# Retention attention followed by a GELU layer pair on one core: first layers of two blocks in token halves, finer activation sums, and POOL's scaling held until a block's sums are done

## The chip, the core and the metric

The kernel runs on one core of a Trainium2 chip. TensorE (PE in the profile) multiplies matrices, with its weight loads on PEld. VectorE (DVE), ScalarE (ACT) and GpSimd (POOL) do this kernel's elementwise work, and the sync engine (SP) issues most of its transfers (96 of the 144 loads of q, k and v; POOL's 48 are the tails). The metric is the time of one execution on the device in us, the median of several runs.

## The reference, cut to what matters

Inputs are q, k and v of 8 sequences, 8 heads, 576 positions and 64 dimensions. The attention is linear, with a causal mask and a decay per head. Its result, 4608 tokens by 512, goes through two layers.

```python
ret = (scale * q @ k.T) * Dmat          # Dmat[i, j] = gamma_h ** (i - j) for i >= j, else 0
x = (ret @ v), heads side by side       # (4608, 512)
h = x @ w_in                            # (4608, 2048)
out = gelu_tanh(h) @ w_out              # (4608, 512)
```

## The kernel before: the parts that the change touches

TensorE works through nine blocks (0 to 8) of 512 tokens. A block is 16 column groups of the first layer (`up`), then the second layer. From block 1 on, the second layer is done with seven products of half matrices instead of eight (`prod`), which needs sums of activations (`act_sums`, on DVE) and of weights (`weight_sums`). Attention work of later sequences is woven into the steps of the blocks. Nothing is rescheduled: each engine gets its instructions in the program's order (in block 2 DVE ran the copy L266 at 121.33 us, behind the sums L440 to L443, which the program has ahead of it and which began at 110.24).

```python
def up(t, fc):                                   # first layer, 512 tokens, 128 columns
    hp = bank("hp", "hp")
    for ct in range(4):
        nc.tensor.matmul(hp..., w_in_sb[:, ct, 128*fc : 128*fc+128], xT[:, o : o + 8, ct, :], ...)
    nc.scalar.activation(out=gT[t][:, fc]..., in_=hp, func=AF.Gelu_apprx_tanh)

def act_sums(t, f0, f1):                         # DVE; both inputs of each lie in SBUF
    nc.vector.tensor_tensor(out=s["1"], in0=a21, in1=a22, op=ALU.add)          # L440
    nc.vector.tensor_tensor(out=s["2"], in0=s["1"], in1=a11, op=ALU.subtract)  # L441
    nc.vector.tensor_tensor(out=a21, in0=a11, in1=a21, op=ALU.subtract)        # L442
    nc.vector.tensor_tensor(out=s["4"], in0=a12, in1=s["2"], op=ALU.subtract)  # L443

# ... blocks 1 on: the sums are issued inside a step, before that step's attention work
            for f in range(NH):
                steps.append(lambda f=f: up(t, f))
                def hi(f=f):
                    up(t, f + NH)
                    if f == 4:
                        act_sums(t, 0, 4)
                    if f == 7:
                        act_sums(t, 4, 8)
                steps.append(hi)
# ...
        for u, s in enumerate(steps):
            s()
            run(t, u)                            # the attention work planned for step u of block t

# scaling of k and q with the decay, on POOL, for sequence b: in block b - 2 from step 16 on
        at(t0, ut[0], lambda b=b: (new_casts(b), new_turned(b)))
        for u, (key, c) in zip(ut, ent):
            at(t0, u, lambda b=b, key=key, c=c, e=eng[key]: cc(b, key, c, e))
```

The "tail" of a sequence is its last 64 positions, loaded by six transfers that POOL issues itself (`load_tail`, L78) and scaled by two smaller products. In blocks 1 to 3 (sequences 1 to 3) transposed k and q come from TensorE through PSUM and are copied to `tt` by DVE (L266); later sequences are transposed by transfers.

## Time and profile before

335.8 us, median of 3 runs (335.27 to 335.86). From the timeline of TensorE, a "block" below lasts from its first first-layer matmul to that of the next block; block 0 counts from the start of the span.

| stretch | us | idle time of TensorE in it that matters |
|---|---|---|
| start and block 0 | 66.55 | 1.88 before the first layer; 1.57 and 2.06 between 41 and 47; 1.3 from 63 to 66.5 |
| block 1 | 33.61 | 0.78 |
| block 2 | 44.78 | 7.27 and 0.89 |
| blocks 3, 4, 5 | 31.61, 33.00, 31.69 | 0.59 in each of blocks 4 and 5 |
| blocks 6, 7, 8 | 32.09, 31.06, 30.81 | none |

The page of the profile, part 1 (busy us, share of the span, instructions) and two rows of part 2 (40 equal slices of 8.4 us, in tenths; PEclk is the granted clock):

```profile
PE 308.9 (92%) x2660; PEld 190.8 (57%) x2660; DVE 191.9 (57%) x303; ACT 167.7 (50%) x322; POOL 130.5 (39%) x175
...
PE   6969869899999748999999999999999999999994
...
PEclk9999998999999959999999999999999999999999
```

TensorE bounds the kernel: no other engine is near it on average. The time that a change could win is where its row is under 9: in five of the first eight slices, and in the 14th to 16th, above all in the 15th, where its busy share is 4 and the clock is 5 (the last slice is the end of the program). The timeline of 109.5 to 123.2 us shows that place (start, duration, engine, line, operation, result and inputs; in brackets the idle time before it and what ended it):

```profile
108.95 1.22 POOL L78 DMA_DIRECT2D lt<-in_v_dram  x2
...
110.18 1.05 POOL L232 TENSOR_TENSOR ck<-ld,sc 128x512 f16<-128x512 f32 x1
110.24 8.52 DVE L440 TENSOR_TENSOR s<-gT 128x1024 f16<-128x1024 f16 x1 [0.84 <-ACT gT L395]
...
111.18 1.05 POOL L232 TENSOR_TENSOR cq<-ld,sc 128x512 f16<-128x512 f32 x1
...
117.18 1.03 POOL L232 TENSOR_TENSOR cq<-ld,sc 128x512 f16<-128x512 f32 x1
118.18 1.05 POOL L232 TENSOR_TENSOR ck<-lt,sc 128x256 f16<-128x256 f32 x1
118.80 0.98 DVE L441 TENSOR_TENSOR s<-s,gT 128x1024 f16<-128x1024 f16 x1
...
121.33 0.68 DVE L266 COPY tt<-tr 128x1024 f16<-128x1024 f16 x1
...
122.06 0.61 PE L288 MATMUL st<-tt 64*128 64x128 f16 x8 [7.27 <-DVE tt L266]
```

Read it from the bottom: TensorE waited 7.27 us for a copy on DVE of 0.68 us. The copy was ready to go at 113, but stood behind four sums, the first of which lasted 8.52 us (the same group has a median of 0.69 in the view of that line). During all of it POOL ran its eight 128x512 products, one every 1.00 us. The wait does not end the loss, as the windows show (window, its length, then busy us and instruction counts of PE, PEld, DVE, ACT and POOL, then PEclk, DMA share and GB/s):

```profile
117.00:122.00 5.00, 0.00 (x0) 0.00 (x0) 4.96 (x5) 0.00 (x0) 5.00 (x7) 0.51 1.15 316
122.00:126.00 4.00, 3.94 (x24) 1.75 (x25) 1.63 (x4) 0.60 (x1) 0.67 (x2) 0.50 1.29 197
126.00:130.00 4.00, 4.00 (x35) 2.51 (x34) 0.97 (x2) 2.78 (x6) 1.23 (x2) 0.83 1.27 202
```

After the wait TensorE ran at half its clock for some five us: in narrower windows the clock is 1.00 from 114.80 to 117.08, 0.50 from 117.10 to 127.32 and 1.00 after, so it was halved 2.3 us into the wait and came back 5.3 us after work began again. Twelve first-layer matmuls took 4.90 us there (at 122.97), against 2.76 at full clock (at 108.54).

In blocks 3 to 5 the same sums meet the same POOL products, but there the two engines take turns: the timeline of DVE in block 4 has each sum at about twice its usual time (1.42 to 1.53 us for 0.69), and POOL's products beside them take 1.49 us instead of 1.04.

```profile
187.06 1.53 DVE L440 TENSOR_TENSOR s<-gT 128x1024 f16<-128x1024 f16 x1
188.62 1.42 DVE L441 TENSOR_TENSOR s<-s,gT 128x1024 f16<-128x1024 f16 x1
```

### The profile page before, as it was taken

Reading aid. Unit: us, or ns where it says so; the run is one execution under the profiler, and the core shown is the slowest. Engines: PE = TensorE matmul, PEld = TensorE weight load, DVE = VectorE, ACT = ScalarE, POOL = GpSimd, SP = SyncE. Lnnn points to the kernel's source line nnn. Section 1 sums busy time; section 2 is a strip of 40 time slices with the busy share of each in tenths; the row PEclk is TensorE's granted clock in tenths of the full one; section 3 lists DMA queues with packets and bytes.
Section 4 is the critical chain, followed back from the end, with each engine's and each line's share of the span. In section 5 each row is a group of like instructions: output and inputs, shape, how many; then the busy total and the mean of one; then the engine's idle time right before and its main releaser. Section 6 shows DMA issues by size and latency. Waiting matters only on the chain.

```text
span 335.2 us, 6603 instructions
## 1 busy us (share of the span) xinstructions
PE 308.9 (92%) x2660; PEld 190.8 (57%) x2660; DVE 191.9 (57%) x303; ACT 167.7 (50%) x322; POOL 130.5 (39%) x175
## 2 busy tenths in 40 slices
PE   6969869899999748999999999999999999999994
PEld 3634335444874326864684478447745864585483
DVE  4854477857554875646643964399345545651352
ACT  6466314778255505447735754674367246713610
POOL 8669368764594961008900980085000000000000
PEclk9999998999999959999999999999999999999999
DMA  8999999999999999875799597304410030003003
GB/s 206 220 349 367 295 248 222 207 236 217 199 215 182 204 269 194 169 203 119 177 192 207 133 177 133 125 2 79 127 63 2 2 124 5 0 2 125 2 0 127
DMA packets 123471, 51.30 MB, mean 153 GB/s; under 512 B 111920, under 2 KB 113968, under 8 KB 123440
## 3 DMA queue, kind: packets, MB, share of 16 engines
q1 hardware_dynamic: 121904, 47.72, 63.1%
q0 software_dynamic: 1536, 3.15, 4.2%
q8 instruction: 21, 0.34, 0.4%
q14 instruction: 10, 0.08, 0.1%
HBM read 36.70 MB, written 9.44 MB: 138 GB/s over the span
## 4 chain that ended last, share of the span: by engine, by line
PE 70%; DVE 12%; DMA 10%; SPq 3%; ACT 2%; issue 2%; POOL 1%; DVEq 0%
PE hp L389 27%; PE opB L458 12%; PE opC L458 9%; PE opA L458 7%; DVE s L440 4%; DMA ld<-in_moe_w_in_dram 4%; PE st L288 3%; PE xs L337 3%; PE op L407 3%; DMA ld<-in_q_dram 2%; SPq L90 2%; PE us L307 2%; DMA ld<-in_moe_w_out_dram 2%; DVE s L441 2%; PE xs L355 2%
## 5 line engine op out<-in xcount | busy, mean ns | idle before, releaser
L389 PE MATMUL hp<-xT,w_in_sb 128*128 128x512 f16 x576 | 135.0, 384 | 2.6 <-ACT xT L376 2.6
L395 ACT ACTIVATE gT<-hp 128x512 f16<-128x512 f32 x144 | 86.2, 598 | 76.0 <-PE hp L389 75.4
L389 PEld LDWEIGHTS <-w_in_sb 128*128 128x128 f16 x576 | 54.3, 99 | 62.5 <-issue 6.7
L232 POOL TENSOR_TENSOR ck<-ld,sc 128x512 f16<-128x512 f32 x31 | 36.4, 1175 | 75.5 <-PE us L307 37.0
L294 DVE TENSOR_TENSOR ret<-st,cm 128x512 f16<-128x512 f32 x64 | 41.2, 685 | 35.4 <-PE st L288 35.4
L458 PEld LDWEIGHTS <-gT 128*128 128x128 f16 x512 | 49.0, 98 | 7.2 <-issue 0.7
L458 PEld LDWEIGHTS <-s 128*128 128x128 f16 x384 | 36.3, 98 | 5.7 <-DVE s L441 1.1
L440 DVE TENSOR_TENSOR s<-gT 128x1024 f16<-128x1024 f16 x16 | 21.1, 1318 | 28.1 <-ACT gT L395 28.1
L328 ACT CAST tbd<-ws 64x256 f16<-64x256 f32 x64 | 25.8, 403 | 14.2 <-DVE ws L323 13.4
L458 PE MATMUL opB<-wt,gT 128*128 128x256 f16 x256 | 30.9, 273 | 0.5 <-DVE ost L472 0.5
L458 PE MATMUL opA<-w_out_sb,gT 128*128 128x256 f16 x256 | 31.0, 273 | 0.0
L232 POOL TENSOR_TENSOR cq<-ld,sc 128x512 f16<-128x512 f32 x24 | 28.1, 1171 | 0.8 <-DMA ld<-in_q_dram 0.6
L288 PE MATMUL st<-tt 64*128 64x128 f16 x288 | 15.2, 221 | 9.1 <-DVE tt L266 8.2
L337 PE MATMUL xs<-ret,cv 128*64 128x128 f16 x288 | 16.8, 225 | 4.8 <-DVE ret L294 3.6
L288 PEld LDWEIGHTS <-tt 64*128 64x128 f16 x288 | 8.2, 95 | 22.8 <-issue 10.0
L337 PEld LDWEIGHTS <-cv 128*64 128x64 f16 x288 | 10.3, 109 | 18.3 <-issue 16.6
L472 DVE TENSOR_TENSOR ost<-k,opC 128x512 f32<-128x512 f32 x16 | 11.0, 687 | 16.4 <-PE opC L458 16.1
L472 DVE TENSOR_TENSOR k<-k,opB 128x512 f32<-128x512 f32 x16 | 11.0, 686 | 15.6 <-PE opB L458 15.6
L376 ACT CAST xT<-xs 128x512 f16<-128x512 f32 x31 | 18.1, 582 | 2.0 <-PE xs L355 1.5
L219 ACT CAST cv<-ld 128x512 f16<-128x512 f32 x24 | 14.0, 616 | 6.5 <-PE xs L337 6.2
L407 PE MATMUL op<-w_out_sb,gT 128*128 128x512 f16 x64 | 16.9, 391 | 0.0
L514 DVE CAST w_out_sb<-ld 128x512 f16<-128x512 f32 x16 | 8.5, 551 | 14.3 <-DMA ld<-in_moe_w_out_dram 14.0
(83 smaller groups left out, 338.0 us busy)
## 6 DMA issues: line engine op xcount, KB each, us to landing
out_dram<-ost SPq DMA_DIRECT2D x17, 512.0 KB, 3.0
ld<-in_q_dram SPq DMA_DIRECT2D x32, 256.0 KB, 5.5
ld<-in_k_dram SPq DMA_DIRECT2D x32, 256.0 KB, 5.2
ld<-in_v_dram SPq DMA_DIRECT2D x32, 256.0 KB, 5.2
ld<-in_moe_w_in_dram SPq DMA_DIRECT2D x16, 256.0 KB, 5.7
ld<-in_moe_w_out_dram SPq DMA_DIRECT2D x16, 256.0 KB, 5.4
lt<-in_k_dram POOLq DMA_DIRECT2D x16, 64.0 KB, 4.5
lt<-in_q_dram POOLq DMA_DIRECT2D x16, 64.0 KB, 6.0
```

The lines of the kernel that those rows point to most:

```text
L232: eng.tensor_tensor(out=dst.rearrange("p (h d) -> p h d", d=D), in0=raw.rearrange("p (h d) -> p h d", d=D), in1=sc[:, s0 : s0 + nh].unsque ...
L288: nc.tensor.matmul(st[hl][:, 128 * p : 128 * p + 128], a["tk"][r, 4 * c + p, :], tq(b, c, p)[r], start=True, stop=True)
L294: nc.vector.tensor_tensor(out=r[:, 0:w], in0=st[hl][:, 0:w], in1=m.rearrange("p n i -> p (n i)"), op=ALU.mult)
L328: cp(out=tbd[b % 2][r, c, :, r], in_=att[b]["w"][r])
L337: nc.tensor.matmul(xs[64 * hl : 64 * hl + 64, 128 * p : 128 * p + 128], a["v"][:, col(c, p, hl)], a["ret"][c, hl][:, 128 * p : 128 * p + 128],
L376: nc.scalar.copy(out=xT[:, g0 : g0 + 2], in_=src)
L389: nc.tensor.matmul(hp.rearrange("p (g t) -> p g t", t=TL), w_in_sb[:, ct, 128 * fc : 128 * fc + 128], xT[:, o : o + TB // TL, ct, :], star ...
L395: nc.scalar.activation(out=gT[t][:, fc].rearrange("p i n -> p (i n)"), in_=hp, func=AF.Gelu_apprx_tanh)
L407: nc.tensor.matmul(op[i], gT[t][:, f, i], w_out_sb[:, f, :], start=(f == 0), stop=(f == NF - 1))
L440: nc.vector.tensor_tensor(out=s["1"], in0=a21, in1=a22, op=ALU.add)
L458: nc.tensor.matmul(op[tag][:, HD * u : HD * u + HD], lhs(f), rhs[:, f], start=(new and u == 0 and f == 0), stop=(f == NH - 1), skip_group_ ...
L472: nc.vector.tensor_tensor(out=o, in0=a, in1=b, op=ALU.add)
```

## The change

Its intent has three parts. Blocks 0 and 1 do their first layer for 256 tokens at a time, so that it can begin before the attention of all 512 tokens is done; the tail of sequence 0 and the chunks of sequence 1 are planned later to fit. The sums of activations are issued in four portions instead of two, after the step's attention work. For sequences 4 to 7, POOL first copies one element of the last sum of the current block (the gate), so that its products cannot start before the sums are done.

```diff
+    def up_half(t, u, f):                      # two column groups for 256 tokens, one bank
+        hp = bank("hp", "hp")
+        for x in range(2):
+            for ct in range(4):
+                nc.tensor.matmul(hp[:, 256*x : 256*x+256]..., w_in_sb[:, ct, 128*(f+x) ...], xT[:, o : o + 4, ct, :], ...)
+        nc.scalar.activation(out=gT[t][:, f : f + 2, 2*u : 2*u + 2, :]..., in_=hp..., func=AF.Gelu_apprx_tanh)
...
-        filler(3)
+        if c + 1 < NC:
+            filler(3)
+        else:
+            up_half(0, 0, 0)
+            up_half(0, 0, 2)
...
+    gate = const.tile([128, 1], F16, name="gate")
...
-    (tail of sequence 0 at steps 0, 8, 10, 13, 14; chunks of sequence 1 at steps 19 to 33 of block 0)
+    (tail at steps 8, 19, 21, 24, 25; chunks from step 21 on, the last one, and the last products of the third, in block 1)
...
         at(t0, ut[0], lambda b=b: (new_casts(b), new_turned(b)))
+        if b >= 4:
+            at(t0, ut[0], lambda t=t0: nc.gpsimd.tensor_copy(out=gate, in_=gs[t]["4"][:, NH - 1, 1, 0:1]))
...
-    plan = {1: (7, 12, 20, 24), 2: (2, 6, 12, 18, 23), 3: (2, 7, 12, 20), ...
+    plan = {1: (7, 12, 15, 20), 2: (2, 7, 11, 17, 22), 3: (2, 7, 16, 22), ...
...
                     up(t, f + NH)
-                    if f == 4:
-                        act_sums(t, 0, 4)
-                    if f == 7:
-                        act_sums(t, 4, 8)
+                    if f % 2:
+                        return lambda: act_sums(t, f - 1, f + 1)
...
         for u, s in enumerate(steps):
-            s()
+            then = s()
             run(t, u)
+            if callable(then):
+                then()
```

More of the change, by code (lines that the diff above doesn't have):

```diff
@@ L397, in up @@
         )
+    def up_half(t, u, f):
+        if t not in gT:
+            gT[t] = sb.tile([128, NF, NI, 128], F16, tag="gT", name="gT", bufs=1)
+        hp = bank("hp", "hp")
+        o = TB * t // TL % NG + 4 * u
+        for x in range(2):
+            for ct in range(4):
+                nc.tensor.matmul(
+                    hp[:, 256 * x : 256 * x + 256].rearrange("p (g t) -> p g t", t=TL),
+                    w_in_sb[:, ct, 128 * (f + x) : 128 * (f + x) + 128],
+                    xT[:, o : o + 4, ct, :],
+                    start=(x == 0 and ct == 0), stop=(ct == 3), skip_group_check=True,
+                )
+        nc.scalar.activation(
+            out=gT[t][:, f : f + 2, 2 * u : 2 * u + 2, :].rearrange("p f i n -> p f (i n)"),
+            in_=hp.rearrange("p (f n) -> p f n", f=2), func=AF.Gelu_apprx_tanh,
+        )
     op = {}
@@ L431, with act_sums @@
     gs = {}
-    def act_sums(t, f0, f1):
+    def act_sums(t, f0, f1, us=slice(0, 2)):
         if t not in gs:
@@ L437, in act_sums @@
         lo, hi = slice(f0, f1), slice(NH + f0, NH + f1)
-        a11, a12, a21, a22 = g[:, lo, :, 0], g[:, hi, :, 0], g[:, lo, :, 1], g[:, hi, :, 1]
-        s = {n: x[:, lo] for n, x in gs[t].items()}
+        a11, a12, a21, a22 = g[:, lo, us, 0], g[:, hi, us, 0], g[:, lo, us, 1], g[:, hi, us, 1]
+        s = {n: x[:, lo, us] for n, x in gs[t].items()}
         nc.vector.tensor_tensor(out=s["1"], in0=a21, in1=a22, op=ALU.add)
@@ L569 @@
     at(0, -12, lambda: nc.gpsimd.memset(tbd[1], 0.0))
-    at(0, -10, lambda: load_tail(0))
+    at(0, -4, lambda: load_tail(0))
     for f in range(NF):
         at(0, -5 + f // 4, lambda f=f: cast_w("o", f))
-    at(0, 0, lambda: [cc(0, key, NC, P) for key in "kqv"])
-    at(0, 8, lambda: turn(0, NC, A.copy))
-    at(0, 10, lambda: score(0, NC))
-    at(0, 13, lambda: av(0, NC))
-    at(0, 14, lambda: put(0, NC))
     at(0, 1, lambda: (new_casts(1), new_turned(1)))
@@ L582 @@
         at(0, 2 + p, lambda p=p, e=e: cc(1, "q", p, e))
+    at(0, 8, lambda: [cc(0, key, NC, P) for key in "kqv"])
     at(0, 11, lambda: weight_sums(0))
@@ L585 @@
         at(0, 15 + p, lambda p=p: turn_q4(1, p, (A.copy, V.tensor_copy)[p % 2]))
-    for c in range(NC):
-        u = 19 + 4 * c
-        at(0, u, lambda c=c: (cc(1, "k", c, P), cc(1, "v", c, P), turn(1, c, A.copy)))
-        if c:
-            at(0, u, lambda c=c: spread(1, c - 1, A.copy))
-        at(0, u + 2, lambda c=c: (score(1, c, "hp"), state(1, c), scan(1, c)))
-        if c:
-            at(0, u + 2, lambda c=c: (av(1, c - 1), put(1, c - 1)))
-    at(0, 33, lambda: (av(1, 3), put(1, 3), spread(1, 3, A.copy)))
+    at(0, 19, lambda: turn(0, NC, A.copy))
+    at(0, 21, lambda: score(0, NC))
+    at(0, 24, lambda: av(0, NC))
+    at(0, 25, lambda: put(0, NC))
+    TU = [(0, 21), (0, 25), (0, 29), (1, 1)]
+    SU = [(0, 23), (0, 27), (0, 31), (1, 3)]
+    VU = [(0, 27), (0, 31), (1, 2), (1, 6)]
+    for c in range(NC):
+        at(*TU[c], lambda c=c: (cc(1, "k", c, P), cc(1, "v", c, P), turn(1, c, A.copy)))
+        at(*SU[c], lambda c=c: (score(1, c, "hp" if c < 2 else "att"), state(1, c), scan(1, c)))
+        at(*VU[c], lambda c=c: (av(1, c), put(1, c), spread(1, c, A.copy)))
     at(1, 1, lambda: weight_sums(4))
@@ L614 @@
         if b == 2:
-            at(1, 2, lambda: load_tail(1))
-            at(1, 14, lambda: tail_casts(1, (P, P, A)))
-            at(1, 14, lambda: load_tail(2))
+            at(0, 31, lambda: load_tail(1))
+            at(1, 9, lambda: tail_casts(1, (P, P, A)))
+            at(1, 12, lambda: load_tail(2))
             at(1, 26, lambda: tail_casts(2, (P, P, A)))
@@ L625 @@
     todo = [(2, 0), (2, 1), (1, NC), (2, 2)] + [(b, c) for b in range(2, B) for c in CH][3:]
-    plan = {1: (7, 12, 20, 24), 2: (2, 6, 12, 18, 23), 3: (2, 7, 12, 20), 4: (1, 6, 11, 17, 23),
-            5: (2, 7, 12, 20), 6: (1, 6, 11, 17, 23), 7: (2, 7, 12, 20)}
+    plan = {1: (7, 12, 15, 20), 2: (2, 7, 11, 17, 22), 3: (2, 7, 16, 22), 4: (1, 6, 11, 17, 22),
+            5: (2, 7, 12, 20), 6: (1, 6, 11, 17, 22), 7: (2, 7, 12, 20)}
     for t, us in plan.items():
@@ L639 @@
     assert not todo
-    for fc in range(NF):
-        up(0, fc)
-        run(0, fc - NF)
+    order = [(u, g) for u, g in ((0, 0), (0, 1), (1, 0), (1, 1), (0, 2), (1, 2), (0, 3), (1, 3))]
+    for n, (u, f) in enumerate([(u, f) for u, g in order for f in (4 * g, 4 * g + 2)]):
+        if n > 1:
+            up_half(0, u, f)
+        run(0, n - NF)
     for t in range(NTB):
@@ L648 @@
             for i0, tags in ((0, "AB"), (2, "CA")):
+                lag = 2 if i0 else 0
                 for f in range(NF):
-                    steps.append(lambda f=f, i0=i0, tags=tags: (
-                        [down_mm(0, i0 + n, f, tags[n]) for n in range(2)],
-                    ))
+                    mm = [(0, f)] + [(1, g) for g in range(max(f - lag, 0), f - lag + 1 if f < NF - 1 else NF)]
+                    steps.append(lambda i0=i0, tags=tags, mm=mm: [
+                        down_mm(0, i0 + n, g, tags[n]) for n, g in mm
+                    ] and None)
                 steps.append(lambda i0=i0: store_pair(0, i0, (A.copy, V.tensor_copy)))
@@ L656, in sums, with half @@
                 return lambda: act_sums(t, f0, f1)
-            for f in range(NH):
+            for u in range(2 if t == 1 else 0):
+                for f in (0, NH, 2, NH + 2, 4, NH + 4, 6, NH + 6):
+                    def half(u=u, f=f):
+                        up_half(t, u, f)
+                        if f in (NH + 2, NH + 6):
+                            return lambda: act_sums(t, f - NH - 2, f - NH + 2, slice(u, u + 1))
+                    steps.append(half)
+            for f in range(0 if t == 1 else NH):
                 steps.append(lambda f=f: up(t, f))
```

## The prediction

> **What bounds the kernel now.** TensorE: 308.9 us busy of 335.2 (busy table). From 145 us on it never rests longer than 0.6 us (its timeline) and a 512-token block costs 31 to 33 us, so I look for gains before that:
> - 21.2 to 23.05: 1.9 us, the first layer of block 0 waits for xT.
> - 41 to 47: 1.57 us on POOL's tail scaling, 2.06 us on the tail's mask on DVE; then the granted clock is 0.60 from 48 to 52 (windows).
> - 63 to 66.5: 1.3 us around the last chunk of sequence 1.
> - 114.8 to 122: 7.27 us, the longest wait. A transposed copy on DVE stands behind an activation sum (L440) that took 8.52 us; the median is 0.69. POOL ran eight scaling products back to back (1.03 to 1.05 us each, 110.18 to 118.2); the sum ended when they did. Then the clock is 0.50 until 126 and 0.83 until 130: twelve first-layer matmuls take 4.9 us where 2.76 is usual. [...]
>
> **What the change does.**
> 1. Gate: POOL's products for sequences 4 to 7 wait for the block's last sum. Sum back to 0.69, copy in time. In block 2: 7.3 (idle) + 0.9 (second wait, 132 us) + 2.5 to 3 (slow clock) = about 11 us, all on the chain. Blocks 3 to 5: 1 to 2 us in all. POOL ends some 4 us later, with about 15 us to spare until the DMA transposes are needed.
> 2. Sums in smaller portions, after the step's attention work: 16 instructions of about 0.4 us for 8 of 0.69. DVE has room (18 to 20 us of 32).
> 3. Token halves: 256-column matmuls, 109 ns apart as in the second layer (eight in 0.87 us), against 216 for 512 columns: no cost to TensorE. Block 0 starts at 20.1 instead of 23.05, in place of three fillers, but then wants the second group of w_in, whose POOL casts end near 24.5: about 1.9 us of stall return. The first layer ends at 36.2 instead of 36.9.
> 4. Tail of sequence 0 and chunks of sequence 1 later. The query transposes at step 15 come at 42.7, but their data lands at 44.6 to 47 (DMA-bound). Then the tail's transpose needs a bank that DVE frees only after its weight sums (about 53). TensorE is at 53 there, as before. One chunk (1.2 us of TensorE) moves into block 1, which starts at 65 (66.55 before) and takes 35 us (33.6), as its sums and weight sums meet POOL work of sequence 2, which isn't gated.
>
> **Sum.** Start of block 1 65.3 + 35.1 + 34.3 (block 2, 44.9 before) + 31.1 + 32.1 + 31.1 + 32.1 + 31.1 + 30.8 = 323.0; the timed runs lie 0.6 above the profile: 323.5 us, 3.7% less. Range 318 to 328.5. Faster by over 2%: 0.93; within: 0.06; slower: 0.01.
>
> **What would show it.** Gate: L440 of block 2 at 0.7 us, no wait of 7 us, clock near 1 at 117 to 130. Step 3: first layer begins near 20, with a stall on POOL's w_in casts. Step 4: waits on DMA and DVE between 42 and 53, block 1 starting at 64 to 66.5.
>
> **What would make it wrong.** The starved sum reappears in block 1 (ungated products of sequences 2 and 3): up to 8 us lost. Later POOL work delays the DMA transposes. Idle TensorE at 42 to 53 costs a longer slow clock; or the weight sums run faster, and 3 us more are gained.

The forecast's sum is 323.0 us for the profile and 323.5 us for the timed runs. "Sum back to 0.69" was the estimate, from the long sum that ended when POOL's products did and from the median of 0.69 us. The 2.5 to 3 us for the slow clock are an estimate too; the twelve matmuls (4.9 us less 2.76) give 2.1 of them.

## The result, and the profile after

324.08 us median of 4 runs (323.68 to 328.66) against 335.83 us before: the ratio is 0.9647, with a 95% interval of 0.9626 to 0.9668. A ratio here is the mean time of one kernel's fast runs over that of the other's fast runs of the same rounds, so it is not quite the ratio of the medians quoted. The run of 328.66 us was slow and is not in it; the median of the three fast runs is 323.86 us.

The stretches, from the timelines of TensorE in the profiled runs:

| stretch | before | predicted | after |
|---|---|---|---|
| start and block 0 | 66.55 | 65.3 | 62.40 |
| block 1 | 33.61 | 35.1 | 36.96 |
| block 2 | 44.78 | 34.3 | 35.26 |
| blocks 3 to 5 | 96.30 | 94.3 | 94.25 |
| blocks 6 to 8 | 93.96 | 94.0 | 93.73 |
| span | 335.2 | 323.0 | 322.6 |

Part 1 and the two rows of part 2 of the page after:

```profile
PE 305.2 (95%) x2785; PEld 199.3 (62%) x2785; DVE 183.6 (57%) x367; ACT 167.2 (52%) x322; POOL 124.9 (39%) x179
...
PE   6889967998999999999999999999999999999994
...
PEclk9799999999999999999999999999999999999999
```

The hole in the 15th slice is gone, and so is the slow clock behind it. The timeline of block 2 after, around the last portion of the sums:

```profile
118.89 0.69 DVE L266 COPY tt<-tr 128x1024 f16<-128x1024 f16 x1 [2.31 <-PE tr L262]
...
119.50 0.41 DVE L458 TENSOR_TENSOR s<-gT 128x512 f16<-128x512 f16 x1
...
120.53 0.40 PE L288 MATMUL st<-tt 64*128 64x128 f16 x8
...
120.62 0.42 DVE L461 TENSOR_TENSOR s<-gT,s 128x512 f16<-128x512 f16 x1
...
121.10 0.19 POOL L634 COPY gate<-s 128x1 f16<-128x1 f16 x1 [12.72 <-DVE s L461]
...
121.24 1.04 POOL L232 TENSOR_TENSOR ck<-ld,sc 128x512 f16<-128x512 f32 x1
```

The sum's portion takes 0.41 us, the copy stands ahead of it, TensorE does not wait, and POOL, after 12.72 us idle, starts as the last sum ends. The windows of the same times:

```profile
117.00:122.00 5.00, 5.00 (x62) 3.81 (x62) 3.08 (x7) 3.98 (x9) 0.90 (x2) 1.00 0.28 105
122.00:126.00 4.00, 4.00 (x49) 3.43 (x47) 2.82 (x5) 2.67 (x7) 4.00 (x5) 1.00 0.69 148
126.00:130.00 4.00, 4.00 (x49) 3.14 (x47) 2.84 (x5) 0.59 (x3) 4.00 (x5) 1.00 1.08 187
```

### The profile page after: what moved, and what is told of

Read it like the earlier page. It is cut to its first block, busy times and chain, and to the rows that moved or that the text cites. A ratio compares the mean times of both kernels' runs of the same rounds, so it can differ in the third digit from the quotient of the medians.

```text
span 322.6 us, 6913 instructions
## 1 busy us (share of the span) xinstructions
PE 305.2 (95%) x2785; PEld 199.3 (62%) x2785; DVE 183.6 (57%) x367; ACT 167.2 (52%) x322; POOL 124.9 (39%) x179
## 4 chain that ended last, share of the span: by engine, by line
PE 74%; DMA 10%; DVE 6%; SPq 4%; issue 2%; POOL 2%; ACT 1%; DVEq 0%; POOLq 0%
PE hp L389 31%; PE opB L476 13%; PE opC L476 9%; PE opA L476 8%; DMA ld<-in_moe_w_out_dram 4%; DMA ld<-in_moe_w_in_dram 3%; PE xs L337 3%; PE st L288 3%; SPq L90 3%; DMA ld<-in_q_dram 3%; PE us L307 2%; PE xs L355 2%; PE tr L262 1%; DVE ret L294 1%; DVE wt L447 1%
## 5 line engine op out<-in xcount | busy, mean ns | idle before, releaser
L389 PE MATMUL hp<-xT,w_in_sb 128*128 128x512 f16 x448 | 103.8, 379 | 0.0
L389 PEld LDWEIGHTS <-w_in_sb 128*128 128x128 f16 x448 | 41.6, 98 | 44.3 <-issue 0.5
L294 DVE TENSOR_TENSOR ret<-st,cm 128x512 f16<-128x512 f32 x64 | 41.2, 685 | 35.9 <-PE st L288 35.8
L232 POOL TENSOR_TENSOR ck<-ld,sc 128x512 f16<-128x512 f32 x31 | 33.2, 1071 | 11.5 <-DMA ld<-in_k_dram 6.8
L406 PE MATMUL hp<-xT,w_in_sb 128*128 128x256 f16 x256 | 30.3, 273 | 1.5 <-ACT gT L412 0.7
L458 DVE TENSOR_TENSOR s<-gT 128x512 f16<-128x512 f16 x32 | 14.6, 456 | 25.9 <-ACT gT L395 24.9
L634 POOL COPY gate<-s 128x1 f16<-128x1 f16 x4 | 0.8, 188 | 69.5 <-DVE s L461 69.5
L406 PEld LDWEIGHTS <-w_in_sb 128*128 128x128 f16 x256 | 24.4, 98 | 5.1 <-POOL w_in_sb L532 1.5
L232 POOL TENSOR_TENSOR cq<-ld,sc 128x512 f16<-128x512 f32 x24 | 25.9, 1078 | 0.1
L337 PEld LDWEIGHTS <-cv 128*64 128x64 f16 x288 | 9.4, 110 | 13.9 <-issue 12.5
```

What stands on the lines that cost most here:

```text
L232: eng.tensor_tensor(out=dst.rearrange("p (h d) -> p h d", d=D), in0=raw.rearrange("p (h d) -> p h d", d=D), in1=sc[:, s0 : s0 + nh].unsque ...
L294: nc.vector.tensor_tensor(out=r[:, 0:w], in0=st[hl][:, 0:w], in1=m.rearrange("p n i -> p (n i)"), op=ALU.mult)
L337: nc.tensor.matmul(xs[64 * hl : 64 * hl + 64, 128 * p : 128 * p + 128], a["v"][:, col(c, p, hl)], a["ret"][c, hl][:, 128 * p : 128 * p + 128],
L389: nc.tensor.matmul(hp.rearrange("p (g t) -> p g t", t=TL), w_in_sb[:, ct, 128 * fc : 128 * fc + 128], xT[:, o : o + TB // TL, ct, :], star ...
L406: nc.tensor.matmul(hp[:, 256 * x : 256 * x + 256].rearrange("p (g t) -> p g t", t=TL), w_in_sb[:, ct, 128 * (f + x) : 128 * (f + x) + 128] ...
```

## The experiments

The theory: nearly all of the gain is the gate, because it keeps DVE's sums, which read two tensors from SBUF, away from POOL's products, which read SBUF too (8.52 us for a sum beside them in block 2, 0.69 in the median). Rivals: that finer sums behind the attention work would have done it; that the token halves carry a good part of it; that any busy POOL, not its reads, holds DVE up. Each ratio below is to the kernel before in the same rounds; the median of before in those rounds was between 335.6 and 336.9 us. Block times are from each run's own timeline. Block 0 varies from profile to profile: the nine profiles with its old code show 65.36 to 67.39 us, the five with the new code 62.25 to 63.23. So a difference of 2 us in that column alone says nothing.

| run | time, us (runs) | ratio (95%) | block 0 | block 1 | block 2 | blocks 3 to 5 |
|---|---|---|---|---|---|---|
| gate only | 325.82 (4) | 0.9695 (0.966 to 0.973) | 66.54 | 33.62 | 35.43 | 94.40 |
| all but the gate | 337.54 (4) | 1.0059 (0.999 to 1.013) | 63.23 | 36.48 | 42.01 | 99.55 |
| finer sums only | 339.48 (4) | 1.0091 (1.003 to 1.015) | 67.39 | 33.39 | 42.64 | 102.39 |
| all but the halves | 324.81 (4) | 0.9664 (0.962 to 0.971) | 65.36 | 33.39 | 35.26 | 94.26 |
| halves only | 342.87 (4) | 1.0159 (1.008 to 1.024) | 62.60 | 41.60 | 45.99 | 96.89 |

### 1. The gate alone

Edit, on the kernel before:

```diff
+    gate = const.tile([128, 1], F16, name="gate")
         at(t0, ut[0], lambda b=b: (new_casts(b), new_turned(b)))
+        if b >= 4:
+            at(t0, ut[0], lambda t=t0: nc.gpsimd.tensor_copy(out=gate, in_=gs[t]["4"][:, NH - 1, 1, 0:1]))
```

> The kernel before with nothing but the gate. Theory (the gate is nearly the whole gain): L440 of block 2 at 0.7 us, no 7.3 us wait, block 2 about 34 to 36 us instead of 44.9, time 325 to 327.5 us. Rival 1 (finer sums that begin earlier do it): the gate alone saves under 3 us, 333 or more. Rival 2 (the gate needs the shifted plan, as the transposed inputs of sequence 4 come later): a new wait in block 3, 328 to 332.

Measured: 325.82 us, block 2 in 35.43 us, the L440 group between 682 and 694 ns throughout. Block 2 gives 9.35 of the 11.3 us between the two spans (335.2 and 323.9), blocks 3 to 5 give 1.9. A wait of 1.19 us for the transposed copy stays in block 2. The theory holds, and no new wait in block 3 showed the old plan to be too early for sequence 4.

### 2. Everything but the gate

Edit: the two gate lines are taken out of the changed kernel.

> The changed kernel without the gate, all else kept. Theory: three of the four portions of the sums of block 2 are issued before POOL has products to do, and only the last meets them; if it starves as before, TensorE waits again for up to 7 us: 329 to 335 us. Rival (the finer sums suffice, since attention work no longer stands behind them): 324 to 326 us.

Measured: 337.54 us, no better than before; slower even than the theory's range. The timeline of block 2 in this run:

```profile
108.13 1.05 POOL L232 TENSOR_TENSOR ck<-ld,sc 128x512 f16<-128x512 f32 x1
...
109.73 6.79 DVE L458 TENSOR_TENSOR s<-gT 128x512 f16<-128x512 f16 x1
...
116.55 0.71 DVE L459 TENSOR_TENSOR s<-s,gT 128x512 f16<-128x512 f16 x1
...
119.01 0.61 PE L288 MATMUL st<-tt 64*128 64x128 f16 x8 [5.53 <-DVE tt L266]
```

A portion of half the size starves as long as a whole one did, until the last of POOL's eight 128x512 products ends at 116.2. I had expected POOL's run to meet only the last portion, because it is written at step 16. But POOL is not held by TensorE's steps and was there at 108, in time for the second portion. In blocks 3 and 4, where turns are taken, the finer sums gain a little (31.33 and 32.06 us against 31.61 and 33.00). Block 5 loses more (36.16 against 31.69): eight small sums that take turns last from 216.5 to 225.2 us there, and TensorE waits 3.38 us for a mask product behind them. Without the gate the finer sums gain nothing in all.

### 3. Finer sums alone

Edit: only the hunks of `hi` and of the step loop above.

> The kernel before with the sums in pairs of column groups, issued after the step's attention work, nothing else. Theory: one portion of 128x512 still meets POOL's run of products and the next transposed copy stands behind it, so at most a few us are saved: 330 to 335. Rival: the copy is ahead of the exposed portion and the wait goes away: 325 to 327.

Measured: 339.48 us, outside both expectations, a little slower than before (interval 1.003 to 1.015). The longest L440 is 8.45 us, now for a 128x512 portion, and TensorE's wait 6.39 us; block 5 takes 37.10 us. So the second run's reading holds without the halves too: in neither run did the sums' new size and place remove the collision.

### 4. All but the halves

Edit: gate, finer sums and the plan of blocks 2 on, put on the kernel before; blocks 0 and 1 have whole first layers and the old schedule. Run twice, the second time in the same rounds as the changed kernel.

> Gate, finer sums and the shifted plan of blocks 2 on, with the first layers and the schedule of blocks 0 and 1 of the kernel before. Theory: from the traces, block 2 starts only 0.8 us later than in the changed kernel (100.2 against 99.4), so the token halves are worth under 1 us: 324 to 325.5. Rival (the 4.15 us won by the start of block 1 are kept): 327 or more.

> The changed kernel again, to be set beside the two runs that follow in the same rounds. 323.5 to 325 us.

> The kernel without the token halves and without the new order of blocks 0 and 1 again. Theory (what the halves win before block 1 is spent inside it): within 1 us of the changed kernel of the same rounds. Rival: over 1 us slower.

Measured: 324.81 us, then 324.50 us (6 runs, ratio 0.9675) beside 324.37 us (6 runs, ratio 0.9648) of the changed kernel. Two of the changed kernel's six runs were slow (329.28 and 329.46 us); the medians of the fast runs are 324.04 us with the halves and 324.50 without, the means differ by 0.7 us, and the intervals overlap. In the two profiles of those rounds the changed kernel starts block 1 2.7 us sooner (62.75 against 65.46) and takes 3.6 us longer in it (36.97 against 33.39). So nearly all that the halves and the new order win in block 0 is spent in block 1; a gain of half a us or so is not excluded.

### 5. The halves alone

Edit: the changed kernel without the gate, with the sums in two portions issued inside the step as before.

> The token halves, the new order of blocks 0 and 1 and the shifted plan, without the gate and with the sums in two portions of 128x1024 issued ahead of the step's attention work, as before. Theory (the gate is the gain): block 1 starts 3 to 4 us sooner, block 1 takes 3 us longer, block 2 keeps a wait of 5 to 8 us: 333 to 337 us. Rival (the halves and the order carry a good part of the gain): 331 or less.

Measured: 342.87 us, slower than expected (0.8 to 2.4% slower than before: the verdict at 2% is unclear). Block 0 keeps its gain (62.60), but block 1 takes 41.60 us: its sums of 128x1024 come ahead of the step's attention work, and TensorE waits 1.16 us for a mask product behind four of them (0.69 us each) and 2.62 us for one behind four that take turns with POOL's products of sequence 3 (0.88 to 1.52 us each), which no gate holds. After that second wait the clock is at 0.50 for 3.4 us. So with the halves the smaller portions behind the attention work are needed: in experiment 2, which has them, block 1 takes 36.48 us, 5.1 less.

### 6. POOL busy without reading SBUF

Edit, on the kernel before; the result is wrong, as sequence 4 gets no scaled k and q:

```diff
     def cast(b, key, c, eng):
...
+            if b == 4 and c < NC:
+                eng.memset(dst, 0.0)
+                eng.memset(dst, 0.0)
+                return
```

> The kernel before with each 128x512 product of sequence 4 on POOL replaced by two 128x512 memsets into the same tile (about 1.1 us): POOL is as busy and writes SBUF, but reads none of it. Gives a wrong result for sequence 4 on purpose. Theory [...]: L440 of block 2 at 0.7 us, no wait over 1.5 us, 325 to 328 us. Rival (any busy POOL holds up DVE, by its writes or otherwise): L440 of several us, 331 or more.

Measured: 327.56 us (4 runs, ratio 0.9728, 0.968 to 0.978). Its timeline, where the sum's line has moved from L440 to L444:

```profile
110.13 0.53 POOL L232 MEMSET cq<- 128x512 f16 x1
110.21 0.69 DVE L444 TENSOR_TENSOR s<-gT 128x1024 f16<-128x1024 f16 x1 [0.84 <-ACT gT L399]
110.71 0.52 POOL L233 MEMSET cq<- 128x512 f16 x1
110.94 0.69 DVE L445 TENSOR_TENSOR s<-s,gT 128x1024 f16<-128x1024 f16 x1
```

POOL is as busy at the same time and writes the same tiles, and the sums take 0.69 us (8.52 us for the first one beside the products). Block 2 takes 35.43 us, the same as with the gate. So the long sum goes with POOL's reading, not with its being busy or its writes. No edit changed DVE's side, but the trace of the kernel before shows a difference: the 64 mask products of 128x512 (L294), with one input in PSUM and one in SBUF, last 674 to 692 ns each, beside POOL's products too (at 160.14), while a product of DVE with both inputs in SBUF (`ws` from `vs`, 0.42 us at 180.46) took 0.93 us beside them at 186.20. The run shows that POOL's reads matter, not why.

### 7. Why one sum starves while others take turns

Blocks 3 to 5 of the kernel before show 1.4 to 1.5 us for a sum beside POOL's products, block 2 shows 8.52. First I tried to let the sum come first, with one small write on POOL (to a tile `late` that nothing reads) ahead of the products, then with four. The question was whether the order of starting matters.

```diff
         at(t0, ut[0], lambda b=b: (new_casts(b), new_turned(b)))
+        if b == 4:
+            at(t0, ut[0], lambda: nc.gpsimd.memset(late, 0.0))      # second run: four of them
```

> The kernel before with one 128x512 memset (about 0.54 us) on POOL ahead of the products of sequence 4, so that the sum, issued at 110.24 us, stands ahead of the first product (then at about 110.7). Theory ([...]the two take turns, as in blocks 3 to 5 where a sum takes 1.4 to 1.5 us): L440 of block 2 at 0.7, the next sums 1.4 to 1.5, the wait shrinks from 7.3 to 2 us or less, 327 to 331 us. Rival (a run of eight back-to-back products starves some sum wherever it starts): a wait of 5 us or more, 334 or more.

> As the run with one memset, which failed to bring the sum ahead of the products (these started at 109.46, the sum at 110.13), now with four memsets, about 2.1 us: products from about 111, sum from 110.2. Theory [...]: first sum 0.7 us, the next 1.4 to 1.5 us each, TensorE's wait 2 us or less, about 328 to 331 us. Rival (in this block a run of products starves a sum wherever it falls): one of L441 to L443 takes 5 us or more, 334 or more.

With one write the run missed its aim: the products started at 109.46 us, the sum at 110.13, and it starved for 7.92 us (336.38 us, ratio 0.9993). With four, all four sums began ahead of the products and took 0.7 us each; at 113.04 it was POOL's product that was stretched (1.51 us). The second set of sums, from 120.42 us on, met the end of the run and took turns (0.69, 1.42, 1.10, 1.10 us). The time was 331.23 us (2 runs, ratio 0.9859, verdict unclear), block 2 39.80 us. The sums that took 0.7 us began ahead of the products (111.02 against 113.04 us), but this run can't tell that from the pause after POOL's transfers, and to begin first was not enough in experiment 3: there the sum began at 110.86 us, ahead of the first product at 110.99, and lasted 8.45 us.

The second idea was those transfers: in block 2 POOL issues six of them directly ahead of its products. Edit, on the kernel before: the transfers of sequence 4 are issued after the eight products.

```diff
-            at(t0, ut[-1] if b == 3 else ut[0] - 1, lambda b=b: load_tail(b))
+            at(t0, ut[-1] if b == 3 else ut[-2] if b == 4 else ut[0] - 1, lambda b=b: load_tail(b))
```

> The kernel before with POOL's six tail transfers of sequence 4 issued after its eight products instead of just ahead of them; in blocks 3 to 5, where turns are taken, they were issued long before or apart. Products start about 106.5 and end about 114.5, so the sum at 110.24 still meets four of them. Theory (the transfers just ahead are what makes POOL win every time): L440 about 1.5 us. Rival (they have nothing to do with it): L440 starves until the products end, about 4 us or more.

Measured: 329.33 us (2 runs, ratio 0.9803, 0.971 to 0.990, verdict unclear), block 2 in 36.89 us. Its timeline:

```profile
108.85 1.04 POOL L232 TENSOR_TENSOR cq<-ld,sc 128x512 f16<-128x512 f32 x1
...
109.49 0.95 DVE L440 TENSOR_TENSOR s<-gT 128x1024 f16<-128x1024 f16 x1 [0.84 <-ACT gT L395]
109.85 1.49 POOL L232 TENSOR_TENSOR ck<-ld,sc 128x512 f16<-128x512 f32 x1
110.47 1.42 DVE L441 TENSOR_TENSOR s<-s,gT 128x1024 f16<-128x1024 f16 x1
```

The sum arrives while POOL's run is under way, as before, and now gets its turn at the next product. How far into the run the sum arrives doesn't explain it: it starved 0.06 us into the run in the kernel before and 1.6 us into it without the gate, while in block 4 of the kernel before a DVE product with two SBUF inputs got its turn 1.4 us into the run (186.20, POOL's run from 184.81). In all five runs where the sum met a run of products that directly followed the six transfers (in one of them with a single write between), it starved; in this run, and in blocks 3 to 5, where the transfers lay many us away (POOL was idle for 17.93 to 23.14 us before those products), it did not. That the transfers' place decides rests on one profile, which also moved POOL's run to an earlier time, so it is likely, not shown; by what means is open.

### 8. A version that is a little better

In block 1 of the changed kernel TensorE waits 1.44 us at 73.76 for the copy of sequence 2's transposes, and the copy stands behind the first portion of the sums (its fourth instruction took 1.26 us beside POOL). Edit, on the changed kernel: this portion is issued two steps later.

```diff
-                        if f in (NH + 2, NH + 6):
+                        if u == 0 and f in (NH + 4, NH + 6):
+                            n = 4 * (f - NH - 4) // 2
+                            return lambda: act_sums(t, n, n + 4, slice(0, 1))
+                        if u == 1 and f in (NH + 2, NH + 6):
```

> The changed kernel with the first portion of the sums of block 1 issued two steps later, behind the transposed copy of sequence 2 on DVE. Theory (the 1.44 us wait at 73.8 us is that copy standing behind the stretched sum): the wait goes, block 1 takes 35.3 to 35.8 us instead of 36.96, time 1 to 1.5 us below the changed kernel. Rival (the copy is late for the weight sums ahead of it, or ScalarE limits block 1 next): under 0.5 us.

Measured, in the same rounds as the changed kernel: 323.34 us (6 runs, ratio 0.9627) against 324.37 (0.9648). The wait is gone and block 1 takes 35.45 us for 36.97, as the theory said. The fast runs differ by 0.7 us in the median (323.34 against 324.04), but the intervals overlap (0.960 to 0.966 and 0.961 to 0.968), so that the wait went is shown, and the gain in the whole time is only likely. It is the fastest version.

## Why the prediction was right, and where it was off

The forecast was 323.5 us and the measurement 324.08, well inside the range. The gain came from where it was predicted: experiments 1 and 2 show that the gate carries it (ratio 0.9695 with the gate alone, 1.0059 with all but the gate), and experiment 6 that the long sum goes with POOL's reads (0.69 us beside writes alone). The total agrees better than its terms: block 0 came out 2.9 us shorter than forecast, blocks 1 and 2 together 2.8 us longer, and that these cancel is luck. (The 0.6 us that I added for the difference of timed and profiled runs should have been 1.7: 324.3 less 322.6 for the same run.)

- Step 1, the gate. "About 11 us" in block 2: the gate alone gave 9.35. The term that was too large is the second wait of 0.9 us, which I counted as saved; with the gate alone a wait of 1.19 us stands there. The changed kernel gained 9.52 us in block 2: that wait is gone too, but two others, of 0.62 us (at 113.5) and 0.39 us (at 130.7), are new. For blocks 3 to 5 "1 to 2 us" was forecast; the gate alone gave 1.9 and the changed kernel 2.05. POOL's later end did no harm: from block 3 on, the list of TensorE's waits after holds one of 0.5 us, near the end, which the kernel before has too.
- Step 2, finer sums: "16 instructions of about 0.4 us" is right (0.41 to 0.42), and DVE has room. What I left out is that without a gate they gain nothing (ratios 1.006 and 1.009 in experiments 2 and 3).
- Step 3, token halves: the first layer began at 20.29 us (20.1 forecast) and ended at 35.86 (36.2). Of the "about 1.9 us of stall" less came: the two waits there are 0.35 and 0.24 us. In a steady stretch TensorE's price was as forecast, eight matmuls of 256 columns every 0.87 us, but over the whole of block 1 the first layer was busy for 15.87 us against 14.91 before (windows of its line), so "no cost" was too low.
- Step 4, the later tail and chunks. TensorE was at the tail's scores at 52.0 us and at the next chunk's transposes at 52.6, with waits on w_out and q data and on DVE before that, as forecast (53). But block 1 started at 62.4 and not at 65, and three terms make up the 2.9 us. The same transposes came at 53.76 before, so TensorE was there 1.1 us sooner and not "as before". From them to block 1 it took 9.8 us instead of 12.8: it waited for 0.3 us in that time instead of 1.3, and it had about 2.0 us less to do, not 1.2, as with the last chunk, the last products of the chunk before it moved into block 1 as well (24 matmuls of `xs`, 12 for each chunk). The slow clock of before is gone, as these windows show, but it does not explain the 1.1 us:

Windows of 48 to 56 us, of the kernel before:

```profile
48.00:52.00 4.00, 4.00 (x22) 2.79 (x22) 3.93 (x4) 1.45 (x3) 4.00 (x5) 0.60 1.06 222
52.00:56.00 4.00, 4.00 (x39) 2.40 (x37) 2.93 (x6) 1.17 (x2) 3.57 (x4) 0.97 1.26 219
```

The same windows of the kernel after:

```profile
48.00:52.00 4.00, 2.45 (x14) 1.18 (x15) 3.93 (x6) 0.65 (x2) 4.00 (x6) 1.00 1.08 221
52.00:56.00 4.00, 3.67 (x45) 2.02 (x45) 2.85 (x6) 0.96 (x2) 4.00 (x7) 1.00 1.05 206
```

Busy time at a lower clock gets less done (twelve first-layer matmuls in 4.90 us at 0.50, in 2.76 at 1.00). Weighted with the clock, TensorE did about the same work in both: 4.00 x 0.60 + 4.00 x 0.97 = 6.3 us before, 2.45 + 3.67 = 6.1 us after. The run with the gate alone, which has block 0 as before, also kept the full clock here, and its transposes still came at 53.76 and its block 0 still took 66.54 us: TensorE waited instead (0.51 us at 50.2, 0.94 us at 52.8, the second for DVE). What fits is the forecast's own warning that the weight sums might run faster: DVE ended the four ahead of the transposes at 52.50 us before, at 52.51 with the gate alone, and at 50.77 after. No run tested this by itself.

```profile
48.00:52.00 4.00, 3.49 (x28) 2.38 (x28) 3.93 (x4) 1.89 (x4) 3.92 (x5) 1.00 1.10 226
52.00:56.00 4.00, 3.06 (x33) 1.62 (x31) 2.93 (x6) 0.72 (x2) 3.57 (x4) 1.00 1.31 219
```

- Block 1 was forecast at 35.1 us and took 36.96. In its windows TensorE is idle for 1.86 us (36.96 less 35.10 busy), against 0.89 before; the view of waits names 1.4 us for the copy behind a stretched sum and 0.3 us for ScalarE. It is also busy for 2.4 us more: for the moved attention work, of which 1.2 us was in the sum and about 2 moved, and for the first layer in halves. The forecast had named the danger of the wait ("the starved sum reappears in block 1") but allowed too little for it in the central number. Experiment 8 removes the largest of these waits.

## What to carry to other kernels

When one instruction lasts over ten times its usual length (here 8.52 us for 0.69), look at what another engine does in exactly that stretch, and then replace the suspect's work by work of the same length without the suspected part (here memsets, which read nothing): that one experiment told reading from being busy. If two engines hold each other up, order them by a cheap dependency (here a copy of 0.19 us on POOL) instead of making the pieces smaller: with more and smaller pieces but no order, this kernel got no faster (ratios 1.0059 and 1.0091). And check where the time that an early stage wins goes: here the next stage spent nearly all of it.

## What the traces show, and what they leave open

- A sum on DVE can lose to POOL every time: one waited through eight POOL instructions in a row (8.52 us, POOL's products 1.00 us apart and not stretched at all), while in other blocks of the same program the two alternate (sums 1.42 to 1.53 us, products 1.49 us).
- What decides between these two cases is open. With POOL's six transfers ahead of its products the sum starved (6.79 to 8.52 us in five runs); with the transfers behind them it took 0.95 us (one run). The means by which they act is open.
- Beside memsets on POOL, which write SBUF and read none of it, the sums with two SBUF inputs took 0.69 us (experiment 6).
- The traces give no length of a wait from which the slow clock follows. In the kernel before, one wait of 2.06 us, after one of 1.57 us a few us earlier, was followed by a clock of 0.60 over four us, while in the kernel after, waits of up to 0.8 us that made TensorE busy for only 2.45 of 4 us left it at 1.00. With the gate alone, waits of 1.98 and 1.19 us at the same place left it at 1.00 too (the windows of 48 to 56 above). So the length of a single wait did not decide here.
